# One low part of a folded weight on GpSimd, placed ahead of three additions for phases

## The chip, the cores and the metric

The kernel runs on one core of a Trainium2 chip. The metric is the device time of one execution in microseconds (us); lower is better. Times of before are the median of three runs. The profile is one execution, recorded by the hardware profiler.

## The reference

Two heads are computed from inputs of 2048 rows and 576 columns and put side by side. Head A is a state-space convolution: for each of 576 channels a long filter is built from complex exponentials and convolved with the input by Fourier transforms. Head B is linear attention with 32 heads of width 18: queries and keys are multiplied by a feature matrix per head, pass through two softmaxes, and the result is multiplied by the output weight `wo`.

```python
# head A
P = jnp.exp((A * dt[:, None])[:, :, None] * pos[None, None, :])
K = 2.0 * jnp.einsum("dn,dnl->dl", C, P).real
y = jnp.fft.irfft(jnp.fft.rfft(u_t, L2) * jnp.fft.rfft(K, L2), L2)[:, :, :L]   # + u * D_skip
# head B
pq, pk = q @ w_phi, k @ w_phi                            # per head
phi = concatenate([softmax(p), softmax(-p)])             # of pq and of pk
kv, z = einsum("bhsf,bhsd->bhfd", phi_k, v), phi_k.sum(rows)
o = (phi_q @ kv) / (phi_q @ z + 1e-6)
b = o.reshape(B, S, D) @ wo
```

## The kernel before, in words

Every operation is recorded first (`Plan.op`), with its engine and the buffers that it reads and writes, and gets a number. Nothing runs then. `Plan.run` walks through the table `ORDER`, a string of these numbers, and issues the operations in just that order. Each engine has a queue of its own and takes its instructions strictly in the order of the table; waits between engines come from the buffers that operations share. So the place of a number in the table decides what stands ahead of what on its engine, and nothing else does. `x` behind a number takes the operation's second engine, `@` names banks of PSUM, and `:8` puts eight small matmuls on zeros (line 237) ahead of it, which keep TensorE (PE in the profile) at work where it would wait.

The work of the two heads is interleaved. Four kinds of it meet at the place of the change.

- The weights of head B are folded anew for the query half: `whole` (lines 375 to 383) brings `wo` in three thirds. Each third is loaded into a buffer of the kind `e`, rounded to the format of the fast matmul by ScalarE (ACT; `vh`, line 382), and the rest that rounding lost is computed by GpSimd (POOL) as `e - vh` (`vl`, line 383). The buffer of that third is free when both have read it.
- The query tiles (`softmax`, lines 427 to 461): VectorE (DVE) takes the maxima of a product in PSUM (line 434), then adds them to it and writes a new buffer `e` (recorded in the helper `tt`, line 314). Only three buffers of the kind `e` exist. The buffer that the second query tile gets is the one that held the first third of `wo`.
- The phases of head A's exponentials (`params` and its `block`, lines 674 to 741): DVE computes `pi`, with a last scaling on line 734, and GpSimd doubles them by integer additions (line 314 through `tt`). The first three of these additions are one of 96 columns and two of 192.
- Groups of the state-space filter: matmuls with `sel` (line 295) compute sizes into banks of PSUM that a query's product has to leave first, ACT takes their exponential (line 811), DVE multiplies (lines 815 to 820), PE multiplies again (`cs`, 64 small matmuls).

```python
def third(c):
    wi = B(stage[c], [128, 5, 192])
    load_rows(wi, src, slice(192 * c, 192 * c + 192), 192)
    op("act", ..., lambda: act.activation(hi.t[:, :, cs], wi.t, AF.Copy), ...)          # L382
    op(eng, ..., lambda: (pool if eng == "pool" else dve).tensor_tensor(
        lo.t[:, :, cs], wi.t, hi.t[:, :, cs].bitcast(F32), op=ALU.subtract), ...)       # L383
```

Of the kernel before, what the change touches and what calls it, by code (L numbers as in the profile page):

```python
# [1017 lines left out]
1524 1525 1526 366 1036x 1529 1531 1532 386 1443@54 1527 1528 1533 1534 1462 1463 1009@06 1464 1035 1011 1444@23 403@6 1466 1467 402 1535 1445@54 1465  # L1018
1472 1010 406 1468 404 394 1473 1043 1537 387 458 1469 1470@2 1474 396@0 395 1536 399 408 1475 1037 405 407 1471x 1476 388@6 1478 1477 1361 1362 389
392 397 390 409@2 393 410 1363 1364 1365 1366 411 1367 1375x 1479@5 1368 1369 1370 1371 1372 1373 1374 413 391 400 1480x 412 414 367@4 371@5 368x 1013  # L1020
994@62 398 995x 372x 996x 1012 415 459@0 364 365 1429 460 369x 374x 1430 373x 370x 375 1431 997 461 462 1432 426@6 425 1538 463 1376 416 1433 1044@24
464x 1434 1435 1688 376 377 1520@01 427 428 1377 1519@67 1539 1046 1045x 155 1436 417 1541 429 526 465 492 418 1542 1014@24:8 430 1540 1545 1544
1521@60:7 1437 466 1543 431 432 1548 1546@7 1438 1653 1016 1550 1654 1549 1692 1547 527@4 467 1551 468 528 1655 1656 1657 433 469 378 1015 419 434 435
436 439@1 441@7 1554 437@2 470 1658 1552 1553 1358@36 440 1028 1555@0 1047 442 1659 1691 438 1378 1556 446@7 1379 1359@21 529 530 531 1381 1380 1382
447 448 1360@03 1383 443@4 444 1661 532 1660 1662 1384 1663 533 1388 1689 1387 1667 1389 471@5 493@6 1664 445 1665 1666 1668 534 1390 1690 535 1385@2
# [69 lines left out]
```

## Time and profile before

| | |
|---|---|
| median of 3 runs | 548.64 us (547.67 to 552.18) |
| span of the profiled execution | 548.1 us |
| TensorE (PE) busy | 526.5 us, 96% |
| VectorE (DVE) busy | 455.4 us, 83% |
| ScalarE (ACT) busy | 382.0 us, 70% |
| GpSimd (POOL) busy | 327.6 us, 60% |
| mean granted TensorE clock | 0.990 |
| DMA share of 16 engines | 61.4% |

The span goes from the first to the last instruction of the profiled execution. The page states no other time for that execution; 548.1 us stands 0.5 us under the median and within the range of the three runs, so sums against the span are carried over to the median as they are. PEld is TensorE's loading of weights, SP the engine that issues the DMAs, and SPq the waits of its queue. A row of a timeline gives start, duration, engine, line, operation, output and inputs with their shapes, the count, and in square brackets how long the engine stood idle ahead of it and whose end released it. A row of a table by windows gives the stretch, its length, PE's busy time in it, the granted clock, the DMA share and the DMA rate in GB/s.

### The profile page before, as it was taken

The numbers are of one execution on the slowest core, as the hardware profiler recorded it, in microseconds if no ns is written. First come the engines' busy times: TensorE is split into PE (matmuls) and PEld (weight loads), VectorE is DVE, ScalarE is ACT, GpSimd is POOL, SyncE is SP. The second block draws the span as 40 slices with busy tenths as digits, with TensorE's granted clock in tenths as the row PEclk, the third lists the DMA queues.
The fourth block names the chain that finished last, engine by engine and source line by source line (L and its number), as shares of the span: only waits on it lengthen the run. The fifth ranks groups of instructions, "written<-read, shape, count | busy, mean of one in ns | idle before, by whom it ended". The sixth has DMA issues, their size and how long they took to land.

```text
span 548.1 us, 19242 instructions
## 1 busy us (share of the span) xinstructions
PE 526.5 (96%) x8192; PEld 439.1 (80%) x8192; DVE 455.4 (83%) x716; ACT 382.0 (70%) x555; POOL 327.6 (60%) x456
## 2 busy tenths in 40 slices
PE   8999999999999897999999999999899999999995
PEld 7999899888888676898788666766689867776984
DVE  6999899898868797799998996999975789787641
ACT  4868798798569897699689987999743454343332
POOL 1073885958778774684568998998343518334300
PEclk9999999999999998799999999999999999999999
DMA  8935711234255669128574489755448889998784
GB/s 229 322 109 171 300 44 33 104 134 135 86 158 190 202 234 298 62 82 238 175 235 137 121 242 290 250 173 172 154 141 258 259 272 307 279 286 256 266 256 149
DMA packets 86163, 107.01 MB, mean 195 GB/s; under 512 B 5698, under 2 KB 70338, under 8 KB 86078
## 3 DMA queue, kind: packets, MB, share of 16 engines
q1 hardware_dynamic: 86078, 105.79, 61.4%
q8 instruction: 64, 1.05, 0.8%
q14 instruction: 21, 0.17, 0.1%
HBM read 61.22 MB, written 44.54 MB: 193 GB/s over the span
## 4 chain that ended last, share of the span: by engine, by line
PE 37%; POOL 7%; DVE 5%; ACT 4%; DMA 4%; issue 2%; SPq 1%; DVEq 0%; ACTq 0%; POOLq 0%
PE psum L295 33%; PE psum L549 3%; POOL cs L757 2%; DMA out_dram<-ot 2%; POOL ac L310 2%; DMA ub<-dram 1%; POOL cs L776 1%; DMA ff<-in_ff_dram 1%; DVE ac L314 1%; PE psum L577 1%; SPq L979 1%; ACT cs L785 1%; DVE cs L314 1%; DVE zo L604 1%; POOL e L310 1%
## 5 line engine op out<-in xcount | busy, mean ns | idle before, releaser
L295 PE MATMUL psum<-wh,x 128*128 128x288 f32 x576 | 125.0, 303 | 0.0
L295 PE MATMUL psum<-vh,x 128*128 128x288 f32 x576 | 123.7, 301 | 1.1 <-DVE ot L300 0.6
L757 POOL TENSOR_TENSOR cs<-cs,pi 128x32 int32<-128x32 int32 (+4 forms) x180 | 108.5, 608 | 8.0
L295 PEld LDWEIGHTS psum<-wh,x 128*128 128x128 f32 x576 | 95.0, 189 | 7.7 <-issue 5.2
L295 PEld LDWEIGHTS psum<-vh,x 128*128 128x128 f32 x576 | 94.0, 188 | 6.2 <-issue 4.0
L295 PE MATMUL psum<-wl,x 128*128 128x288 f32 x320 | 94.2, 296 | 0.0
L295 PE MATMUL psum<-vl,x 128*128 128x288 f32 x320 | 93.7, 294 | 0.0
L811 ACT ACTIVATE psum<-psum 128x512 f32<-128x512 f32 x108 | 59.9, 587 | 17.5 <-PE psum L295 17.1
L295 PEld LDWEIGHTS psum<-wl,x 128*128 128x128 f32 x320 | 60.7, 190 | 0.0
L295 PEld LDWEIGHTS psum<-vl,x 128*128 128x128 f32 x320 | 60.2, 188 | 0.0
L310 POOL TENSOR_TENSOR x<-zo,x 64x128 fp32r<-64x128 f32 (+1 forms) x30 | 24.4, 814 | 47.6 <-ACT x L394 44.0
L310 POOL TENSOR_TENSOR e<-e,small 128x1152 f32<-128x1152 f32 (+1 forms) x24 | 41.2, 1720 | 14.4 <-DVE small L450 6.8
L815 DVE TENSOR_TENSOR cs<-psum,cs 128x1024 f32<-128x1024 f32 x36 | 43.5, 1211 | 3.6 <-ACT psum L811 3.6
L310 POOL TENSOR_TENSOR e<-small,e 128x576 f32<-128x576 f32 x26 | 30.6, 1177 | 25.5 <-DVE small L437 13.0
L816 DVE TENSOR_TENSOR cs<-psum,cs 128x1024 f32<-128x1024 f32 x36 | 43.6, 1213 | 1.5 <-PE psum L295 1.3
L295 PEld LDWEIGHTS psum<-kvb,fT 126*128 126x128 f32 (+1 forms) x320 | 38.3, 188 | 7.2 <-issue 3.4
L295 PE MATMUL psum<-ub,ff 64*32 64x288 f32 x1024 | 40.5, 409 | 3.1 <-DVE fT L300 0.9
L295 PEld LDWEIGHTS psum<-cs 128*32 128x32 f32 x2304 | 34.9, 111 | 10.2 <-issue 3.7
L295 PE MATMUL psum<-cs 128*32 128x64 f32 x2304 | 40.8, 223 | 1.5 <-DVE cs L820 0.7
L295 PE MATMUL psum<-kvb,fT 126*128 126x133 f32 (+1 forms) x320 | 41.6, 280 | 0.1
L440 ACT ACTIVATE e<-e 128x1152 f32<-128x1152 f32 x32 | 37.0, 1164 | 2.7 <-POOL e L310 1.3
L781 ACT ACTIVATE cs<-cs 128x1040 f32<-128x1040 int32 x36 | 38.3, 1063 | 0.6 <-POOL cs L776 0.4
(156 smaller groups left out, 1118.9 us busy)
## 6 DMA issues: line engine op xcount, KB each, us to landing
dram<-zi SPq DMA_DIRECT2D x32, 576.0 KB
ub<-dram SPq DMA_DIRECT2D x64, 288.0 KB
dram<-zo SPq DMA_DIRECT2D x32, 288.0 KB
zo<-in_xT_dram SPq DMA_DIRECT2D x24, 320.0 KB
zi<-dram SPq DMA_DIRECT2D x12, 576.0 KB
ub<-in_u_dram SPq DMA_DIRECT2D x16, 288.0 KB
xd<-x SPq DMA_DIRECT2D x8, 576.0 KB
x<-xd SPq DMA_DIRECT2D x8, 576.0 KB
```

The lines of the kernel that those rows point to most:

```text
L295: pe.matmul(o, l, r, start=start, stop=stop, skip_group_check=skip)
L310: op(eng, [c_dve(n[0]) if e == "dve" else c_pool(n[1]) for e in eng], lambda e: (dve if e == "dve" else pool).tensor_tensor(dst(), a(), b( ...
L314: op(eng, c_dve(n) if eng == "dve" else c_pool(n), lambda: e.tensor_tensor(dst(), a(), b(), op=alu), r=r, w=w, with_=with_, lock=eng == "p ...
L440: op("act", c_act(1152) + 40, lambda: act.activation(e.t, e.t, AF.Exp), r=[e], w=[e], table="exp")
L549: pe.transpose(tp.t[0:m, j - j0, :], e.t[:, sign, 7 * g:7 * g + GRP[g], :].rearrange("p h f -> p (h f)"), ident.t)
L577: pe.transpose(tp.t[:, k], of(128 * k), ident.t)
L604: op("dve", c_dve(n), lambda: dve.scalar_tensor_tensor(p_at(), m_at(), 0.5, t_at(), op0=ALU.mult, op1=ALU.add), r=[t, rest], w=[p])
L757: op("pool", c_pool(2 * n * W), lambda n=n, j=j: pool.tensor_tensor(x()[:, :, :, n:2 * n], x()[:, :, :, 0:n], pi.t[:, j:j + 2, gs].bitcast ...
L781: act.activation(cs.t[:, 1], cs.t[:, 1].bitcast(I32), AF.Sin, scale=TURN)
L811: op("act", c_act(512), lambda b=b: act.activation(b.t, b.t, AF.Exp), r=[b], w=[b], table="exp")
L815: op("dve", c_dve(64 * W), lambda: dve.tensor_tensor(F(), both(M.t), F(), op=ALU.mult), r=[M, cs], w=[cs])
L816: op("dve", c_dve(64 * W), lambda: dve.tensor_tensor(E.t[:, :, :, 32:64], both(up.t), cs.t[:, :, :, 0:32], op=ALU.mult), r=[up, cs], w=[E])
```

## The change

One number moves in `ORDER`: 417, the low part of the first third of `wo` (line 383). It stood behind 1433, 1044, 464, 1434, 1435 and others; it now follows 416, the rounding of the same third by ScalarE, at once. 1433, 1434 and 1435 are the three additions for phases on GpSimd. Nothing is added or removed.

```diff
-... 375 1431 997 461 462 1432 426@6 425 1538 463 1376 416 1433 1044@24
-464x 1434 1435 1688 376 377 1520@01 427 428 1377 1519@67 1539 1046 1045x 155 1436 417 1541 429 526 ...
+... 375 1431 997 461 462 1432 426@6 425 1538 463 1376 416 417 1433
+1044@24 464x 1434 1435 1688 376 377 1520@01 427 428 1377 1519@67 1539 1046 1045x 155 1436 1541 429 526 ...
```

On GpSimd, where the additions for phases (`pi`) meet the first third's low part (`vl`), the queue differs so:

```order
 L757 TENSOR_TENSOR cs<-cs,pi 128x16x2x8
 L757 TENSOR_TENSOR cs<-cs,pi 128x16x2x16
+L383 TENSOR_TENSOR vl<-e,vh 128x5x192
 L314 TENSOR_TENSOR pi<-pi 128x96
 L314 TENSOR_TENSOR pi<-pi 128x192 x2
-L383 TENSOR_TENSOR vl<-e,vh 128x5x192
 L310 TENSOR_TENSOR e<-small,e 128x576
 L314 TENSOR_TENSOR pi<-pi 128x192
```

The low part moved past three additions; the rest of GpSimd's queue is as it was, and so is the whole order on PE, DVE, ACT and SP. On VectorE, where the scaling of the phases (line 734) and the query tile's write of the reused buffer `e` (line 314, input from PSUM) stand, the rows before and now are:

```order
L437 TENSOR_REDUCE small<-e 128x32
L734 TENSOR_SCALAR pi<-pi 128x384
L310 TENSOR_TENSOR e<-small,e 128x576
L434 TENSOR_REDUCE small<-psum 128x32
L314 TENSOR_TENSOR e<-psum,small 128x576
L300 COPY zi<-psum 128x576
L437 TENSOR_REDUCE small<-e 128x32
```

No row moved here. What changed is the wait of the row `e<-psum,small`: it waits for GpSimd's `vl` because that reads the buffer it will overwrite, and that `vl` now stands three places earlier in GpSimd's queue.

More of the change, by code (lines that the diff above doesn't have):

```diff
@@ L1020 @@
 392 397 390 409@2 393 410 1363 1364 1365 1366 411 1367 1375x 1479@5 1368 1369 1370 1371 1372 1373 1374 413 391 400 1480x 412 414 367@4 371@5 368x 1013
-994@62 398 995x 372x 996x 1012 415 459@0 364 365 1429 460 369x 374x 1430 373x 370x 375 1431 997 461 462 1432 426@6 425 1538 463 1376 416 1433 1044@24
-464x 1434 1435 1688 376 377 1520@01 427 428 1377 1519@67 1539 1046 1045x 155 1436 417 1541 429 526 465 492 418 1542 1014@24:8 430 1540 1545 1544
+994@62 398 995x 372x 996x 1012 415 459@0 364 365 1429 460 369x 374x 1430 373x 370x 375 1431 997 461 462 1432 426@6 425 1538 463 1376 416 417 1433
+1044@24 464x 1434 1435 1688 376 377 1520@01 427 428 1377 1519@67 1539 1046 1045x 155 1436 1541 429 526 465 492 418 1542 1014@24:8 430 1540 1545 1544
 1521@60:7 1437 466 1543 431 432 1548 1546@7 1438 1653 1016 1550 1654 1549 1692 1547 527@4 467 1551 468 528 1655 1656 1657 433 469 378 1015 419 434 435
```

## The prediction

> **What bounds the kernel now.** I read the page first: the busy times and the clock row.
>
> ```profile
> PE 526.5 (96%) x8192; PEld 439.1 (80%) x8192; DVE 455.4 (83%) x716; ACT 382.0 (70%) x555; POOL 327.6 (60%) x456
> PEclk9999999999999998799999999999999999999999
> ```
>
> PE is busy nearly throughout, and its clock dips in just two slices of 13.7 us, the 16th and 17th, which is 206 to 233 us. The change acts there. So next came the waits from 205 to 216 us (who waited for whom, us in total, times, longest).
>
> ```profile
> PE psum L295 <- DVE e L314: 2.8, 1, 2.8
> DVE e L314 <- POOL vl L383: 2.6, 1, 2.6
> ```
>
> This is a chain of three engines: PE waits for VectorE's write of a buffer `e`, and VectorE waits for GpSimd's `vl`. The timelines of the engines show it in time.
>
> ```profile
> 206.45 0.99 ACT L382 ACTIVATE vh<-e 128x960 fp32r<-128x960 f32 x1
> ...
> 202.37 2.88 POOL L757 TENSOR_TENSOR cs<-cs,pi 128x64 int32<-128x64 int32 x4
> 210.31 1.88 POOL L314 TENSOR_TENSOR pi<-pi 128x96 int32<-128x96 int32 x3 [5.06 <-DVE pi L734]
> 212.14 2.21 POOL L383 TENSOR_TENSOR vl<-e,vh 128x960 fp32r<-128x960 f32 x1
> ...
> 208.75 0.55 DVE L314 TENSOR_TENSOR pi<-pi,ot 128x384 f32<-128x384 f32 x1
> 209.88 0.35 DVE L734 TENSOR_SCALAR pi<-pi 128x384 int32<-128x384 f32 x1
> 211.01 0.76 DVE L434 TENSOR_REDUCE small<-psum 128x32 f32<-128x576 f32 x1
> 214.38 0.76 DVE L314 TENSOR_TENSOR e<-psum,small 128x576 f32<-128x576 f32 x1 [2.61 <-POOL vl L383]
> 215.05 0.75 DVE L300 COPY zi<-psum 128x576 f32<-128x576 f32 x1
> ...
> 211.76 0.62 PE L295 MATMUL psum<-sel,mg 64*128 64x512 f32 x2
> 215.19 0.50 PE L295 MATMUL psum<-sel,mg 64*128 64x512 f32 x2 [2.81 <-DVE e L314]
> ```
>
> GpSimd stands idle from 205.25 to 210.31, waiting for the phases of line 734, with `vl` behind the additions, although `vl`'s input `vh` is ready at 206.45 + 0.99 = 207.44. `vl` ends at 214.35, VectorE starts at 214.38, PE at 215.19. What that costs PE beyond its own 2.81 us is in the table by windows, cut at the edges of the clock's dip.
>
> ```profile
> 188.45:191.87 3.42, 2.04 (x16) 1.00 0.63 175
> ...
> 208.93:212.35 3.42, 3.42 (x26) 1.00 0.94 259
> 212.35:215.76 3.41, 0.53 (x4) 1.00 0.94 340
> 215.76:219.17 3.41, 3.32 (x16) 0.50 1.04 316
> 219.17:222.59 3.42, 3.42 (x55) 0.50 0.75 247
> 222.59:226.00 3.41, 3.41 (x43) 0.50 0.00 0
> 226.00:229.41 3.41, 3.41 (x29) 1.00 0.00 0
> ```
>
> Behind the gap PE runs at half clock for 226.00 - 215.76 = 10.24 us while it is busy all the time. A window with 0.53 us of work was followed by half clock; one with 2.04 us of work (188.45) was not.
>
> **The change part by part.** *The wait that goes.* `vl` waits for `vh` alone now: start about 207.48, end 207.48 + 2.21 = 209.69. VectorE's write of `e` stands behind L434, which ends at 211.01 + 0.76 = 211.77. So its wait of 2.61 us is gone: it would start at 211.80, 2.58 us earlier. The additions still wait for line 734, which ends at 210.23, and `vl` is out of their way by then, with 0.5 us to spare. If that cover were gone they would be late by the overrun, and the next who needs GpSimd is the query's `e`, at 216.59 in the old time. No DMA is issued by the moved step, and neither SP's queue nor ACT's is passed.
>
> *What `vl` now collides with.* In its new place VectorE works beside it; in the old one VectorE stood still for it. Rows of VectorE and GpSimd at another place show what can happen (duration in ns as minimum, median, maximum).
>
> ```profile
> L310 DVE TENSOR_TENSOR zo<-zo x5: 757/758/1228, 343.9 to 507.0; 128x576 f32<-128x576 f32 x5
> L314 DVE TENSOR_TENSOR e<-psum,small x32: 689/757/761, 24.4 to 512.2; 128x576 f32<-128x576 f32 x32
> ...
> 452.36 1.23 DVE L310 TENSOR_TENSOR zo<-zo 128x576 f32<-128x576 f32 x1
> ...
> 451.81 1.16 POOL L310 TENSOR_TENSOR e<-small,e 128x576 f32<-128x576 f32 x1 [11.00 <-DVE small L437]
> ```
>
> A VectorE operation with both inputs in SBUF, normally 0.76 us, took 1.23 where a GpSimd operation had begun before it: it ended at 453.59, as if it had begun at 452.83, that is 0.14 before the GpSimd operation's end at 452.97. The form with an input from PSUM never took over 0.761 in 32 cases, so it does not suffer. Beside the new `vl` (207.48 to 209.69) one VectorE operation has both inputs in SBUF: `pi<-pi,ot` at 208.75. By the row it will act as if begun at 209.69 - 0.14 = 209.55, so all of VectorE behind it is 0.80 late, line 734 and the additions too. The write of `e` then starts at 211.80 + 0.80 = 212.60: the gain on VectorE is 214.38 - 212.60 = 1.78 us. Bounds: 2.58 if nothing is held up; 1.64 if it is held to the very end of `vl`. I take 1.78.
>
> The Trainium skill's page "SBUF — State Buffer", section "Who interferes with whom", has a rule that speaks against this change: VectorE with two SBUF inputs and a GpSimd instruction that reads SBUF exclude each other, and the second is fully blocked until the first finishes. The trace agrees but for 0.14 us (1.23 against 0.76 us in the row at 452.36); by the rule to the letter the gain on VectorE would be the 1.64, and the total below 4.6 instead of 4.7.
>
> *The clock.* With the write of `e` at 212.60 to 213.36, PE's `sel` starts 1.78 earlier, at 213.41, so PE's gap from 212.38 is 1.03. It ends at 213.91, and the zero matmuls wait for `zi` until 214.07, 0.16 more. PE's work from 212.35 to 215.76 is then about 3.41 - 1.19 = 2.2 us, above the 2.04 that kept the clock. So I expect full clock. What is late next is VectorE, for which I need its stretch up to PE's next matmuls with `cs`, and the speeds of PE at both clocks.
>
> ```profile
> 218.94 1.23 DVE L816 TENSOR_TENSOR cs<-psum,cs 128x1024 f32<-128x1024 f32 x1 [0.15 <-ACT psum L811]
> 225.29 0.68 DVE L818 TENSOR_TENSOR cs<-psum,cs 128x512 f32<-128x512 f32 x1
> 228.55 0.76 DVE L434 TENSOR_REDUCE small<-psum 128x32 f32<-128x576 f32 x1 [2.58 <-PE psum L295]
> 229.70 0.76 DVE L314 TENSOR_TENSOR e<-psum,small 128x576 f32<-128x576 f32 x1 [0.39 <-PE psum L549]
> ...
> 203.23 0.40 PE L295 MATMUL psum<-wh,x 128*128 128x288 f32 x1
> 210.90 1.24 PE L295 MATMUL psum<-ub,w 64*128 64x288 f32 x8
> 221.49 1.94 PE L295 MATMUL psum<-cs 128*32 128x64 f32 x64
> 223.35 0.61 PE L295 MATMUL psum<-wh,x 128*128 128x288 f32 x1
> 228.35 1.25 PE L549 MATMUL psum<-ident,e 128*126 128x128 f32 x10
> 236.74 1.10 PE L295 MATMUL psum<-cs 128*32 128x64 f32 x64
> ```
>
> PE's 64 `cs` matmuls need L816, which ends at 220.17; 1.78 earlier is 218.39. Before, they began only at 221.49, held by half clock. Now: begin 218.4, 1.03 to the next matmul at full speed (the 1.10 of 236.74 less the 0.07 in which the next already runs), then the query product of 28 matmuls, which takes half of the 7.67 us that 56 took from 203.23 to 210.90, 3.84. It ends at 223.3 instead of 228.35: 5.05 us earlier. VectorE is at work without a gap worth naming from 214.38 to 225.97, so there it gains only the 1.78 and is free at 224.19. Then L434 and the next write of `e`, 0.79 later, at 224.98 instead of 229.70: 4.72 us. The second lane is the tighter; it releases the banks and the softmax of the next query tile, so I take **4.7 us**, with 5.05 where PE has slack to its data.
>
> *What could eat it.* Everything behind hangs on PE and VectorE; PE's next larger wait is a single one of 1.0 us.
>
> ```profile
> PE psum L549 <- DVE ac L314: 1.0, 1, 1.0
> ...
> 208.67 2.65 SPq L407 DMA_DIRECT2D x<-xd x2
> ...
> x<-xd SPq DMA_DIRECT2D x8, 576.0 KB
> ...
> 359.12:362.53 3.41, 2.36 (x59) 1.00 1.04 317
> ```
>
> The query product needs its rows `x`, whose two loads of 576 KB are issued by 211.3. At the latest they have landed by 222.6, where the DMA share falls to 0.00. The DMA engines moved 259 x 3.42 + 340 x 3.41 + 316 x 3.41, some 3.1 MB, from 208.9 to 219.2, against 1.2 MB for the two, so I estimate them as there by 219.4, when the product would begin.
>
> Sum: 548.64 - 4.7 = **543.9 us**; the profiled span would be 543.4.
>
> **The rivals.** *B, no collision*: `pi<-pi,ot` gets by. Then 2.58 on VectorE, `cs` from 217.6, product done at 222.5 (5.85 earlier), the write of `e` at 224.18 (5.52 earlier): 543.1. For it: not every such pair in the trace need be slowed. Against it: the row at 452.36.
>
> *C, the wait goes but the clock is no gain*: the half clock comes anyway, because 2.2 us of work is little above 2.04, or the timed runs of before did not have it. Then only 1.78 remains: 546.9. Against it: the profiled execution with the dip took as long as two of the three runs. The Trainium skill's page "TensorE: Matmul & The Clock Gate", Part 1, "What's actually happening", says that the clock halves after an idle window of about 3.4 us and that these windows run free of the kernel; the trace differs, since a window with 0.53 us of work sufficed. By that rule a gap of 2.81 us would cost no clock, and the result would be this rival's 546.9.
>
> *D, `x` is late*: it lands at 222.6, the product ends at 222.6 + 3.84 = 226.4, 1.9 earlier than before: 546.7. For it: other loads share the same engines then; against it: the 3.1 MB.
>
> *E, slower*: all times behind move by 4.7 us, and the half clock comes at another place instead, most likely at 359.12 to 362.53, PE's poorest window behind the change but for the kernel's last (2.36 us of work). It decides once that window falls under a limit between 0.53 and 2.04. Small matmuls follow there, beside which the clock stayed low for two busy windows above; four windows would cost 13.65 / 2 = 6.8 us: 548.64 - 4.7 + 6.8 = 550.7.
>
> **How the numbers follow.** Chances: forecast 0.58, B 0.15, C 0.15, D 0.04, E 0.08. The forecast's own range is 543.0 to 544.8 (gains of 5.05 and 4.35, the latter if VectorE's L434 alone sets the pace, with half a microsecond of scatter). The range for 8 in 10 takes in B and C: 542.8 to 547.2. About 1%, here 5.5 us, is what a measurement can tell from no change. Faster by that needs 543.15 or less: half of B and a fifth of the forecast's case, 0.20. Slower by it needs 554.1: a longer form of E, 0.03. Within 1%: 0.77.
>
> **What would show it.** `vl` at about 207.5, with 2.2 us; `pi<-pi,ot` stretched from 0.55 to 1.35; the additions at about 211.1; the write of `e` at 212.6 with no wait for `vl`; no slice with a low clock; the `cs` matmuls about 3.1 us earlier, with PE waiting for L816, and the transposes 5 us earlier than 228.35. Wrong it is if the clock still dips, if `pi<-pi,ot` keeps its 0.55, or if the gain at 228 us is larger than at the end.

## The result, and the profile after

Over 22 executions each, the changed kernel took 545.38 us (540.9 to 550.45) and the kernel before 548.11 us on the same chip. The ratio is 0.9946, with a 95% interval of 0.9927 to 0.9966: 0.5% faster, which is within 1% of no change. 543.9 us had been forecast. The median lies in the wide range (542.8 to 547.2), above the forecast's own (543.0 to 544.8), and about midway between the forecast and rival C's 546.9.

One sentence ahead of this is wrong: the three additions for phases have the numbers 1434, 1435 and 1436; 1433 is VectorE's scaling on line 734. What moved, and past what, is shown correctly there by the rows of GpSimd's queue.

The profiled execution of the changed kernel has a span of 543.3 us, and its own time is 545.11 us. The busy times and the clock row of its page:

```profile
PE 521.5 (96%) x8192; PEld 435.9 (80%) x8192; DVE 455.9 (84%) x716; ACT 382.1 (70%) x555; POOL 328.8 (61%) x456
PEclk9999999999999999999999999999999999999999
```

PE is busy 5.0 us less, with the same instructions, and the two slices with a low clock are gone. ScalarE, GpSimd, VectorE and PE at the place of the change, from the timelines:

```profile
206.19 0.99 ACT L382 ACTIVATE vh<-e 128x960 fp32r<-128x960 f32 x1
...
207.25 2.29 POOL L383 TENSOR_TENSOR vl<-e,vh 128x960 fp32r<-128x960 f32 x1 [2.27 <-ACT vh L382]
210.96 1.88 POOL L314 TENSOR_TENSOR pi<-pi 128x96 int32<-128x96 int32 x3 [1.43 <-DVE pi L734]
...
208.70 1.25 DVE L314 TENSOR_TENSOR pi<-pi,ot 128x384 f32<-128x384 f32 x1
210.54 0.34 DVE L734 TENSOR_SCALAR pi<-pi 128x384 int32<-128x384 f32 x1
211.47 0.74 DVE L434 TENSOR_REDUCE small<-psum 128x32 f32<-128x576 f32 x1
212.31 0.76 DVE L314 TENSOR_TENSOR e<-psum,small 128x576 f32<-128x576 f32 x1
216.88 1.23 DVE L816 TENSOR_TENSOR cs<-psum,cs 128x1024 f32<-128x1024 f32 x1 [0.16 <-ACT psum L811]
224.55 0.76 DVE L314 TENSOR_TENSOR e<-psum,small 128x576 f32<-128x576 f32 x1
...
213.12 0.50 PE L295 MATMUL psum<-sel,mg 64*128 64x512 f32 x2 [0.80 <-DVE e L314]
213.79 1.03 PE L237 MATMUL psum<-ident,zero 64*128 64x256 bf16 x8 [0.16 <-DVE zi L300]
218.16 1.10 PE L295 MATMUL psum<-cs 128*32 128x64 f32 x64 [0.89 <-DVE cs L816]
223.03 1.25 PE L549 MATMUL psum<-ident,e 128*126 128x128 f32 x10
```

`vl` follows `vh` at once. VectorE's write of `e` (212.31) no longer waits for it, `pi<-pi,ot` is stretched to 1.25 us, PE's gap is 0.80 instead of 2.81 us, and the `cs` matmuls wait for VectorE instead of being held by a slow clock. This profile ran ahead of the one of before already ahead of the change, VectorE's row on line 732 by 0.27 us (206.63, now 206.36) and ScalarE's `vh`, on which `vl` now hangs, by 0.26, though PE by only 0.05 (210.90, now 210.85). The shifts are counted from the 0.27: the write of `e` is 2.07 - 0.27 = 1.80 us earlier, the next one (229.70, now 224.55) 5.15 - 0.27 = 4.88. Counted from PE they would be 2.02 and 5.10. The table by windows, at the edges on which the clock is decided in this execution (stretch, length, PE busy, granted clock, DMA share, GB/s):

```profile
207.03:210.44 3.41, 3.41 (x28) 1.00 1.01 307
210.44:213.86 3.42, 2.46 (x17) 1.00 0.94 347
213.86:217.27 3.41, 3.41 (x25) 1.00 1.03 299
```

So in the profile nearly everything came as forecast, yet the median moved by 2.7 us and not by 4.7. The experiments ask why.

### The profile page after: what moved, and what is told of

It reads as the page before. It is cut to its first block, busy times and chain, and to the rows that moved or that the text cites. A ratio compares the mean times of both kernels' runs of the same rounds, so it can differ in the third digit from the quotient of the medians.

```text
span 543.3 us, 19242 instructions
## 1 busy us (share of the span) xinstructions
PE 521.5 (96%) x8192; PEld 435.9 (80%) x8192; DVE 455.9 (84%) x716; ACT 382.1 (70%) x555; POOL 328.8 (61%) x456
## 4 chain that ended last, share of the span: by engine, by line
PE 69%; DVE 13%; DMA 7%; ACT 4%; issue 3%; SPq 2%; POOL 1%; DVEq 0%; ACTq 0%; POOLq 0%
PE psum L295 63%; PE psum L549 3%; DMA ff<-in_ff_dram 2%; DMA dram<-zi 2%; PE psum L237 2%; DVE ac L314 1%; DVE cs L816 1%; SPq L979 1%; PE psum L577 1%; DMA cs<-dram 1%; DVE e L310 1%; DMA ub<-dram 1%; DVE e L314 1%; DVE small L434 1%; DVE small L437 1%
```

## The experiments

Two theories stood at the start. *The clock theory*: the wait on VectorE is worth about 1.8 us and the half clock behind it about 3 more. *Rival C*: only the wait counts in the timed runs, and the half clock is either rare in before or comes anyway in after. Each ratio below is against the kernel before in executions on the same chip.

### Both kernels again

Before unchanged, and the changed kernel unchanged three times, to see how much one profile stands for.

```diff
 (no edit)
```

> The kernel before once more, for the granted clock of each of its executions. Theory (the gap of 2.8 us makes the clock drop, in windows that do not follow the kernel): most executions show a mean clock of 0.988 to 0.993, which is one stretch of some 10 us at half clock, and those with 0.997 or more are about 3 us shorter; the median is 548.1. Rival (the drop in the profile was chance, and the wait alone is the gain): at most a third of the executions show it.

> The changed kernel once more, for a profile in another phase of the clock's windows. Theory: no half clock at 212 to 226 us; where an execution has a mean clock under 0.994, the drop lies at another gap of PE, and costs about 3 us; median 545.4. Rival: the drop still comes at 212 to 226 us in those executions.

> The changed kernel a third time, beside the others of this call. Theory: mean clock 0.995 to 0.9965, executions of 0.9965 and above at 544.5 to 545.5, median 545.4 to 546.0, 0.45 to 0.55% under the kernel before. Rival (the gain is that of the profiled pair): 543.7, 0.9% under it.

> The changed kernel beside after_early, on the same chip. Theory: median 545.4 to 546.1, executions of mean clock 0.9965 and above the most frequent kind; where the profile shows half clock, it is not at 212 to 226 us. Rival: half clock at 212 to 226 us.

Before came to 546.85 us in 10 executions (ratio 0.9977, 0.9945 to 1.001); the changed kernel to 545.96 (0.9942, 0.9912 to 0.9972), 546.07 (0.9952, 0.9928 to 0.9976) and 544.98 (0.9943, 0.9919 to 0.9967). The first of these is the measure of chance: the same kernel twice differs by 0.2%, and its median missed the 548.1 that had been expected.

Counted as above, from VectorE's row on line 732, the write of `e` is 1.80, 1.81 and 1.79 us earlier than in before in the other three profiles of the changed kernel, and the next one 4.87, 4.87 and 4.83. The same count gives 0.28 and 0.53 for the second profile of before, where nothing was changed; so much is chance in it.

The second profile of before shows the same wait and the same dip. Its windows stand at other times relative to the work, and a 0.63 us window is followed by three at half clock:

```profile
211.09:214.51 3.42, 0.63 (x6) 1.00 0.95 343
214.51:217.92 3.41, 3.40 (x16) 0.50 1.01 302
217.92:221.33 3.41, 3.41 (x34) 0.50 0.85 275
221.33:224.75 3.42, 3.42 (x64) 0.50 0.02 7
224.75:228.16 3.41, 3.41 (x28) 1.00 0.00 0
```

The second and the third profile of the changed kernel have no half clock at the place of the change. The fourth (own time 547.93, span 546.2) is the slowest of its 12 executions and the most useful. Its windows:

```profile
211.36:214.78 3.42, 1.94 (x17) 1.00 0.98 352
214.78:218.19 3.41, 3.41 (x17) 0.50 1.06 317
218.19:221.60 3.41, 3.41 (x82) 1.00 0.60 207
279.63:283.04 3.41, 1.11 (x9) 1.00 0.57 198
283.04:286.45 3.41, 3.18 (x56) 0.50 0.02 8
```

The clock does dip behind the shortened wait here, which the run's theory had ruled out and its rival had named: only 1.94 us of PE's work lie in the window. But it dips for one window, not three, and costs next to nothing: 12.28 us pass from one write of `e` to the next (212.19 to 224.47), against 12.24 in the first profile, since VectorE is busy there almost without a gap and sets the pace. A second dip at 283 us stands in no other profile. It follows a long wait of PE for a load. PE's 64 matmuls with `ub,ff`, from the timelines of both profiles of before, of the changed kernel, and of its fourth profile:

```profile
286.78 2.24 PE L295 MATMUL psum<-ub,ff 64*32 64x288 f32 x64 [0.82 <-ACT cs L785]
```

```profile
285.62 2.24 PE L295 MATMUL psum<-ub,ff 64*32 64x288 f32 x64 [0.57 <-DMA ub<-dram]
```

```profile
281.84 2.24 PE L295 MATMUL psum<-ub,ff 64*32 64x288 f32 x64 [1.18 <-DMA ub<-dram]
```

```profile
283.27 3.71 PE L295 MATMUL psum<-ub,ff 64*32 64x288 f32 x64 [2.52 <-DMA ub<-dram]
```

In before either ScalarE's result or the load of `ub` is last. In the changed kernel it is the load in three profiles (1.18, 0.96 and 2.52 us) and ScalarE's result in the third (0.83). So the wait for the load isn't new, and that the change made it longer isn't shown: SP issues these loads some 5 us earlier too (from 276.28, now from 270.99). In the fourth profile the place costs 1.70 us more wait than in the first of before and 3.71 - 2.24 = 1.47 for the half clock behind it: 5.22 us of lead (VectorE's row at 284.31 of before) become 2.04 (at 289.22).

### Is the half clock worth its 3 us?

25 zero matmuls (line 237) are put into PE's gap in the kernel before, so that the wait stays and the clock is kept.

```diff
-... 1435 1688 376 377 1520@01 427 ...
+... 1435 1688 376 377 1520@01:25 427 ...
```

> The kernel before, with 25 matmuls on zeros on PE ahead of the sel matmuls at 211.8 us, so that PE works through the gap while VectorE still waits for vl. Theory: no half clock behind it; PE then waits for VectorE's L816 (ends 220.2) and the transposes come at about 225.2 instead of 228.35, 3 us earlier; the gain is 2 to 3 us, median 545 to 546. Rival (the clock plays no part in the median): within 0.5 us of the kernel before, 547.6 to 548.6.

The median was 550.37 us, ratio 1.0029 (0.9994 to 1.0065): no gain, a miss for the clock theory's number and outside the rival's too. The profiled execution (own time 547.53) shows the theory's mechanism and a new stall. The clock was 1.00 throughout, and between VectorE's rows at 216 and at 229.7 of before the lead grew from 0.40 to 3.46 us: 3.06 us for the clock. But PE stops elsewhere, from the timeline:

```profile
342.10 1.16 PE L295 MATMUL psum<-ub,ff 64*32 64x288 f32 x21 [1.17 <-issue]
```

1.17 us for nothing that the profile shows ("issue"), in the middle of 32 like matmuls. In the profiles of the two kernels no such stall is longer than 0.27 us. That the added instructions bring it is a guess from one profile. One stall of this size doesn't explain 550.37, and the executions reach 555.16; what the rest is stays open. So the gap was filled once more without adding instructions: the matmuls with `sel` in the gap are done 8 times (14 more, on the same data), and 14 of the zero matmuls at the start of the kernel are left out.

```diff
-                for r, rs in enumerate((lo, hi)):
+                for r, rs in [*enumerate((lo, hi))] * (8 if g == 16 and k == 1 else 1):
...
-0 1 2 3 1097 ... 6 27 7@0:49 20 ...
+0 1 2 3 1097 ... 6 27 7@0:35 20 ...
```

> The kernel before, with the sel matmuls that PE runs ahead of its gap at 211.8 us done 8 times over instead of once (14 more), and 14 fewer zero matmuls at the very start, so that PE's instruction count behind the gap is as before. VectorE still waits for vl. Theory (the gap costs the clock, and the 25 extra instructions pairs of the run before_warm cost waits for instructions later): no half clock at 212 to 226 us, no waits of over 1 us of PE for nothing visible, transposes about 3 us earlier, mean clock 0.995 or more, median 545.0 to 546.5. Rival (work on PE in the gap does harm by itself): the median is 549 or more again.

547.43 us, ratio 0.9979 (0.9957 to 1.0002): between the theory and its rival, and not clear of no change. In the profile the clock is 1.00, PE waits 1.28 us for the write of `e` where it waited 2.81, and the lead grows between the same two rows by 3.06 us, the same as with the zero matmuls. Here, too, a stall without a visible cause moved in, at another place:

```profile
188.47 0.71 PE L295 MATMUL psum<-e,v 128*19 128x36 f32 x60 [1.27 <-issue]
```

What follows: the half clock behind the wait costs about 3 us at this place. Between those two rows 13.32 and 12.82 us pass in the two profiles of before, and 10.26 in both of these, so it is 2.6 to 3.1. The medians don't show it: neither kernel that keeps the clock by extra work on PE is clear of before, and why they don't get the gain is open.

### Half of the change

`vl` moves behind the first of the three additions only (417 behind 1434), so that it can't meet VectorE's `pi<-pi,ot`.

```diff
-464x 1434 1435 1688 ... 155 1436 417 1541 429 ...
+464x 1434 417 1435 1688 ... 155 1436 1541 429 ...
```

> Half of the change: vl stands behind the first of the three additions only. Theory: vl runs at about 211.1 to 213.4, the write of e starts at 213.4 instead of 214.38, PE's gap is 1.8 instead of 2.8 us; the wait gives 1.0 us, and the half clock comes in fewer executions or for less long (mean clock between 0.991 and 0.9965); median 546.5 to 547.5, between the two kernels. Rival (any smaller gap keeps the clock): mean clock 0.9965, median 545.6 to 546.

> The half change once more, for its profile. Theory: vl at about 211.1, held by VectorE's e<-small,e until 210.9, the write of e at 213.4, PE's gap 1.8 us, so PE works 1.4 to 1.6 us in a window of 3.41 us that holds the gap whole; with half clock behind it if the limit lies above that, without if below.

546.64 us, ratio 0.9978 (0.9949 to 1.0007), not clear of no change; one of the 12 executions took 1692 us, and without it the median is 546.57. The one execution of the second run took 549.33, and its profile shows `vl`, VectorE and the window of PE that decides on the clock:

```profile
210.57 2.26 POOL L383 TENSOR_TENSOR vl<-e,vh 128x960 fp32r<-128x960 f32 x1
...
208.22 0.55 DVE L314 TENSOR_TENSOR pi<-pi,ot 128x384 f32<-128x384 f32 x1
212.87 0.76 DVE L314 TENSOR_TENSOR e<-psum,small 128x576 f32<-128x576 f32 x1 [1.63 <-POOL vl L383]
...
210.48:213.89 3.41, 1.58 (x12) 1.00 0.95 361
213.89:217.30 3.41, 3.39 (x17) 0.50 1.02 299
```

`pi<-pi,ot` keeps 0.55 us, so its 1.25 in the changed kernel does come from `vl` beside it. The wait goes down by 2.61 - 1.63 = 0.98 us, but the clock dips as in before (three windows). This profile was 0.59 ahead on line 732; counted from there the lead is 0.82 us at 216 and 1.07 at 229.7, against 4.88 in the changed kernel. Most of the difference comes with the clock, the rest with the part of the wait that is left.

### Without the collision

Both VectorE operations of the phases go ahead of `vl`: 1432 (`pi<-pi,ot`) and 1433 (line 734) behind 1431, in the changed kernel.

```diff
-... 1431 997 461 462 1432 426@6 425 1538 463 1376 416 417 1433
+... 1431 1432 1433 997 461 462 426@6 425 1538 463 1376 416 417
```

> The changed kernel, with VectorE's pi<-pi,ot and L734 moved ahead of L434, so that they are over when vl begins. Theory (the two exclude each other): pi<-pi,ot takes 0.55 us again instead of 1.25, the write of e starts 0.7 to 1.1 us earlier than with the change alone, and the time falls by 0.4 to 1.1 us, to 544.3 to 545.0. Rival (the stretching is hidden behind other work): the write of e is earlier, the time stays at 545.4.

> The changed kernel with pi<-pi,ot and L734 ahead of L434 once more, beside the changed kernel on the same chip. Theory (the collision costs 0.8 us of VectorE, and the drops of the clock at 188 to 195 us that it showed fall on either kernel alike): 0.4 to 1.0 us faster than the changed kernel, 544.6 to 545.4. Rival (the collision costs nothing to the end): equal to it within 0.4 us.

546.77 us (0.9985, 0.9956 to 1.0014) and 546.88 (0.9968, 0.9943 to 0.9993): 0.8 us above the changed kernel each time, so theory and rival both missed. In the first profile `pi<-pi,ot` took 0.56 us, PE's gap fell to 0.30, and the clock dipped at another place, ahead of the change, behind a window from 189.13 with 1.75 us of work; why this version isn't faster stays open. In the second the collision was back, with another partner, GpSimd's row first:

```profile
206.72 2.29 POOL L383 TENSOR_TENSOR vl<-e,vh 128x960 fp32r<-128x960 f32 x1 [2.28 <-ACT vh L382]
...
206.20 0.56 DVE L314 TENSOR_TENSOR pi<-pi,ot 128x384 f32<-128x384 f32 x1
206.79 2.44 DVE L734 TENSOR_SCALAR pi<-pi 128x384 int32<-128x384 f32 x1
```

`vl` began 0.07 us ahead of line 734, which then took 2.44 instead of 0.35 us: it ended 0.22 after `vl`. So an operation with one input in SBUF is held as well, even where `vl` is ahead by less than 0.1 us. Then only 1432 was moved, which leaves VectorE the maxima of a bank of PSUM (line 434) and the additions to them while `vl` runs.

```diff
-... 1431 997 461 462 1432 426@6 425 1538 463 1376 416 417 1433
+... 1431 1432 997 461 462 426@6 425 1538 463 1376 416 417 1433
```

> The changed kernel with pi<-pi,ot alone moved ahead of L434; L734 stays where it was, after vl's end. Theory (in the run after_clear2 it was L734 that met vl and took 2.4 us instead of 0.35): pi<-pi,ot 0.55 and L734 at most 0.6 us, the write of e 0.4 to 0.7 us earlier than in the changed kernel as counted from L732, median 0.3 to 0.7 us under the changed kernel of this call. Rival (what VectorE gains here is lost again behind 440 us, where the transfers fill the DMA engines): equal to the changed kernel within 0.3 us.

> The changed kernel with VectorE's pi<-pi,ot moved ahead of the statistics of the second bank, once more, to tell whether it is better than the changed kernel itself. Theory: the collision's 0.6 us on VectorE is saved, and the window behind PE's wait holds more work, so the clock falls less often: a median of 544.3 to 545.0 against 545.5 of the changed kernel, and about three in four executions with a mean granted clock of 0.996 or more (30 of 56 of the changed kernel). In the profile pi<-pi,ot takes 0.56 us and the write of e starts near 211.75. Rival: the 0.6 us are given back behind 280 us, where loads set the pace, and the twelve earlier executions were a lucky draw: a median of 545.3 to 546 and about half of the executions at 0.996 or more.

544.77 us (0.9941, 0.9912 to 0.997) and 544.41 (0.9917, 0.9886 to 0.9948). From the first profile:

```profile
207.28 2.28 POOL L383 TENSOR_TENSOR vl<-e,vh 128x960 fp32r<-128x960 f32 x1 [2.29 <-ACT vh L382]
...
206.75 0.56 DVE L314 TENSOR_TENSOR pi<-pi,ot 128x384 f32<-128x384 f32 x1
209.48 0.35 DVE L734 TENSOR_SCALAR pi<-pi 128x384 int32<-128x384 f32 x1
211.74 0.76 DVE L314 TENSOR_TENSOR e<-psum,small 128x576 f32<-128x576 f32 x1
...
210.37:213.78 3.41, 2.96 (x22) 1.00 0.97 314
```

The write of `e` is another 0.57 us earlier (the line 732 rows of the two profiles differ by 0.02), and the window across PE's gap holds 2.96 us of work here. In the second profile line 734 began 0.7 us earlier than the end of `vl` and took 0.94 us, and the clock dipped behind a window at 189 us, ahead of the change:

```profile
189.22:192.63 3.41, 1.64 (x10) 1.00 0.75 237
192.63:196.04 3.41, 3.38 (x18) 0.50 0.05 19
196.04:199.46 3.42, 3.42 (x72) 0.50 0.89 292
```

All 18 executions have a median of 544.49 us, against 545.53 for the 56 of the changed kernel; the means are 1.06 us apart (resampled 95% interval 0.19 to 1.91). That comparison mixes chips. On the one chip where both ran, the medians are 544.77 and 544.98, which is what the rival said, "equal to the changed kernel within 0.3 us". So it is the lowest median of all versions, by 0 to 0.2%, and that it is better than the changed kernel isn't settled.

### What the single executions say

Each execution is listed with its mean granted clock. A dip of three windows costs 10.24 / 2 = 5.12 us of clock in some 548, 0.0093 of the mean; one window costs 0.0031. So the executions sort roughly by dips, and this table tells the two theories apart. It holds all executions of the three kernels whose clock is on record, with the count and the median (mean) in us; two of before that took 628 and 979 us are left out:

| mean granted clock | before | changed kernel | 1432 moved as well |
|---|---|---|---|
| up to 0.992 | 75: 549.38 (549.24) | 11: 548.05 (547.39) | 2: 545.80 (545.80) |
| 0.993 to 0.995 | 29: 546.79 (546.94) | 15: 546.34 (546.21) | 3: 547.20 (546.53) |
| 0.996 and above | 7: 547.01 (547.01) | 30: 545.00 (544.85) | 13: 543.98 (544.04) |
| all | 111: 548.66 (548.50) | 56: 545.53 (545.71) | 18: 544.49 (544.65) |

Before has a low clock in 75 of 111 executions, the changed kernel in 11 of 56. Taken at the changed kernel's shares, before's means give (11 x 549.24 + 15 x 546.94 + 30 x 547.01) / 56 = 547.43. So of the 548.50 - 545.71 = 2.79 us between the means, 548.50 - 547.43 = 1.07 come with the clock and 547.43 - 545.71 = 1.72 at equal clock. The last is near the size of the wait (1.80). But before's highest group has only 7 executions: resampled, the 95% intervals of the two parts are about 0.5 to 1.8 and 0.9 to 2.4, so the split shows that both parts count and not how much of each. Which gap a low mean clock comes from is known only for the profiled executions.

## Why the prediction was right or wrong

- *The wait that goes, with the collision*: right. 1.80 us on VectorE against 1.78; `pi<-pi,ot` 1.25 us against 1.35, and 1.64, 1.62 and 1.78 in the other three profiles, where it began earlier beside `vl`. In all four it ended as if begun 0.14 us ahead of `vl`'s end, just the 0.14 taken from the row at 452.36. That 1.80 meets 1.78 so closely is partly luck (the count differs by 0.28 between the two profiles of before): `vl` took 2.29 us instead of 2.21, and L434, which in before began 0.87 us after the row ahead of it, now began 0.66 after it, a slack that had not been counted. The additions came 0.65 us later, as forecast, and GpSimd stood idle for 1.63 us behind them.
- *The clock stays*: right in three of the four profiles of the changed kernel, and closer than it was put. The limit had been set between 0.53 and 2.04 us of work in a window. The runs put dips behind 1.58, 1.64, 1.75 and 1.94 us. The windows across PE's gap in the four profiles held 2.46, 2.07, 2.09 and 1.94 us, and the last one dipped. So the 2.2 us that had been worked out was little above the limit, and where the window falls is chance. In the fourth profile the dip was harmless.
- *The second lane, 4.72 us*: right, 4.83 to 4.88 in the four profiles. The query product ended 5.32 us earlier in the first (228.35 to 223.03), or 5.05 less the head start of 0.27, as put (5.27 if counted from PE's 0.05). The rows `x` were in time, since the product followed the `cs` matmuls without a wait: rival D is out.
- *Rival B* (no collision) is refuted by the 1.25 us, *rival E* by the sign. In the fourth profile a dip did come at another place, at 283 us and not at 359, but behind a wait for a load that stands in before as well; that the change brought it isn't shown.
- *The sum, 548.64 - 4.7*: this step was off, by 2 us. It carried the gain of the profiled execution over to the median as it was, because the page's 548.1 us "stands 0.5 us under the median" and was taken for the execution's time. But an execution's time is 1.7 to 1.9 us above its span in every run here (545.11 for 543.3, 547.93 for 546.2, 544.56 for 542.8). So the profiled execution of before took about 549.9 us, 1.3 above the median of 548.64 and above two of the three runs. It is one with a dip, of mean clock 0.990; 36 of before's 111 executions have a mean clock above 0.992, so no dip that long. The profiled one of after took 545.11. Its difference, 549.9 - 545.1 = 4.8, is the 4.7 of the forecast, and the forecast span of 543.4 came to 543.3. The medians are 548.11 and 545.38, 2.73 apart: before has a clock that low only in some two thirds of its executions, and the changed kernel still dips in some. By the prediction's own sign, "if the gain at 228 us is larger than at the end", this part was wrong. That the median lies in the wide range all the same is because the range took in rival C.
- *Rival C* is thereby half true, for a reason that it named, "or the timed runs of before did not have it". What spoke against it in the prediction, "the profiled execution with the dip took as long as two of the three runs", was the same misreading of the span.
- *What is late next*: VectorE was named; the load of `ub` at 281 us, on which the fourth profile lost 3.2 us, was not. Behind 440 us the leads of the single profiles scatter: from 440 to 538 us of before they go from 5.03 to 4.98, 5.24 to 5.59, 5.95 to 4.14 and 2.60 to 1.91. The DMA engines are nearly full there, in the changed kernel (stretch, length, busy time of PE, PEld, VectorE, ScalarE and GpSimd, clock, DMA share, GB/s):

```profile
440.00:460.00 20.00, 19.46 (x336) 14.00 (x334) 18.14 (x30) 9.68 (x17) 9.84 (x7) 1.00 0.96 298
460.00:480.00 20.00, 18.56 (x303) 14.26 (x304) 15.90 (x26) 7.56 (x14) 10.67 (x9) 1.00 0.94 293
```

In before the same stretches have shares of 0.94 and 0.93. PE waits for loads there for 2.3, 1.3, 4.4 and 0.2 us in the four profiles of the changed kernel, and 0.7 and 1.7 in the two of before. So a single execution can lose 2 us there without any half clock (the third took 546.55 at a mean clock of 1.000), but that the change loses its gain there isn't shown.

The Trainium skill's page "TensorE: Matmul & The Clock Gate", Part 1, "What's actually happening", was cited for windows of about 3.4 us that run free of the kernel. The traces agree on that: the clock changes only on a raster of 3.41 us, and its place against the work differs from one execution to the next (edges at 212.35, 211.09 and 211.36 in three profiles). They differ on the idle window: windows with 0.53 to 1.94 us of work were followed by half clock.

## What to carry to other kernels

A wait on TensorE of 2 to 3 us can cost more than itself when it empties half a clock window, and with a wait near the limit it is drawn anew in each execution: read the mean granted clock of many executions before you price it from one profile, and add to the span what lies around it. Here shortening the wait paid and filling it with dead matmuls did not, though the filled gap kept the clock too. When an operation is moved beside another engine's, see which two touch SBUF together, and give the other engine work from PSUM for that time.

## What was not expected of the hardware

- Half clock came behind windows that were half full: 1.11, 1.58, 1.64, 1.75 and 1.94 of 3.41 us busy. From 20 to 530 us of eleven profiles every window with 2.01 us or more kept the clock, and every one with less lost it but one. The limit isn't sharp in busy time as recorded, as this one of 1.75 kept it:

```profile
209.66:213.07 3.41, 1.75 (x13) 1.00 0.92 318
213.07:216.48 3.41, 2.48 (x20) 1.00 1.07 310
```

- It lasted one window (fourth profile), two (192.63 to 199.46) or three (before), though PE was busy nearly all of that time. What sets the number isn't settled; the two shortest windows ahead, 0.53 and 0.63 us, had three, but so had one of 1.58.
- PE stood still for 1.17 and 1.27 us with no visible cause, once in each of the two profiles where matmuls had been added or taken out elsewhere in the program; in the other eleven no such stall reached 0.4 us between 14 and 500 us.
- VectorE's `TENSOR_SCALAR` with a single input was held by a GpSimd operation for 2.1 us.
